# Attention weights times v in blocks of 64 keys on either half of the partitions, each half for its own queries

## The chip, the cores and the metric

The kernel runs on one NeuronCore of a Trainium2 chip. Its engines are TensorE (PE in the profile, with weight loads as PEld), VectorE (DVE), ScalarE (ACT), GpSimd (POOL) and SyncE (SP, which here only issues transfers). The metric is the device time of one execution in microseconds. Three runs of the kernel before took 1031.42, 1033.16 and 1033.86 us, median 1033.16.

## The reference

Attention with a threshold for 8 batches of 8 heads, 576 tokens and 64 values a head: each query keeps only the keys whose score lies within tau of its best. Then a block with an activation on all 4608 tokens. Everything is float32.

```python
scores = scale * np.matmul(q, k.transpose(0, 1, 3, 2))
thresh = np.max(scores, axis=-1, keepdims=True) - tau
scores = np.where(scores >= thresh, scores, -1000000000.0)
attn = np.exp(scores - np.max(scores, axis=-1, keepdims=True))
attn = attn / (np.sum(attn, axis=-1, keepdims=True) + 1e-09)
attn_out = np.matmul(attn, v)
x = attn_out.transpose(0, 2, 1, 3).reshape(4608, 512)
h = x @ w_in                                   # 512 -> 1024
solu = h * softmax(h)
ln = (solu - mean) / np.sqrt(var + 1e-06) * g_ln
out = ln @ w_out                               # 1024 -> 512
```

## The kernel before, in words

**Units and slots.** Two heads that lie next to each other are a pair (hp, four a batch). A unit is one pair with 256 queries (kind 0 or 1), or, as kind 2, the last 64 queries of all four pairs of a batch: nine units a batch, 72 in all. A unit is made in two slots of 128 queries (r = 0, 1), so there are 144 slots, and the main loop (line 764) runs one round a slot and some more at the end. Everything is written out in program order (manual_schedule); each engine takes its instructions in that order.

**A round's scores.** TensorE writes the scores of the slot's two heads into the PSUM tiles s0 and s1 (line 414). VectorE takes each row's maximum (430) and makes the threshold of it (434), ScalarE pushes what is below the threshold far down (443) and takes the exponential with its sum (453), GpSimd divides by the sum in the round after (460 to 463). Before the scores, in the same PSUM tiles, stand items: transposes of q, k or the second block's u by TensorE (282), at most seven of 64 columns.

**Turning the weights.** The product with v needs keys on the partitions. VectorE's transpose turns 32x32 blocks only (475): a row group of 32 queries stays where it is, and T holds, for each of the 18 key blocks, 32 keys by 32 queries. T has two buffers. When both slots of a unit are turned, SP issues 16 transfers (485) that move blocks to other partitions: the 18 key blocks are cut into four runs of 4 or 5 (STARTS, COUNTS), run c goes to partitions 32c to 32c + 31, for each of the four query groups a. In wT, then, four blocks of keys stand on 128 partitions, at five places j, of which the fifth is filled for one half of the partitions only.

**The product with v.** attend (491) multiplies on the four 64x64 quadrants of TensorE: the row half r holds keys, the column half h is the head. For each j there are up to four matmuls of 64 keys by 256 queries (516), 18 a unit; for the fifth place (j = 4, with v's tail in its own tile ve) only the row half z has keys. Each half of the keys collects its sum in a PSUM bank of its own. In the next round attended (522) brings the two together: ScalarE copies the lower half's sum to xh (537), VectorE adds the upper half's (538). Only then do the two banks of this PSUM tile return to the list pairs_free, which holds two tiles, p0 and p1, for all of pv, h_ps and o_ps.

**The second block.** A tile of 128 tokens takes four quarters, one a round: h_ps in two (569), then o_ps of the tile before in two (674). After the second quarter VectorE takes the row maximum hm (582), ScalarE the exponential u (588), VectorE the product (594) and later the statistics (604); TensorE turns u in the rounds after (282). After the last slot both products are made in the plain form (560, 665) with tp_u (645) as the transpose of u. Output goes out by SP (704).

**What sets the order around the change.** A unit whose second slot is s is due for its product in round s + LAG_PV (709); the loop (816) takes it when no tile is in work or the quarter is one of the two with h_ps. In a group of four rounds, then, two units are multiplied in the h_ps rounds, after h_ps. A new tile is taken up in the round after its last unit's product. blocks for slot s stand in round s + 1, at its end. SP's queue holds, in program order, block transfers, outputs and the loads of q, k and v of the next batch (load_at, 731).

Of the kernel before, what the change touches and what calls it, by code (L numbers as in the profile page):

```python
# [8 lines left out]
F32 = mybir.dt.float32  # L9
# [11 lines left out]
def kernel(  # L21
# [63 lines left out]

    STARTS = ((0, 5, 10, 14), (0, 4, 8, 13))
    COUNTS = ((5, 5, 4, 4), (4, 4, 5, 5))

    halves = {}
    ends = {}  # L90
    tails = {}
    pairs = {}
# [47 lines left out]
    def load_v(b, hf):  # L140
        d = halves.setdefault((b, hf), {})
        hs = slice(4 * hf, 4 * hf + 4)
        d["v"] = loads.tile([P, 4, 4, D], F32, tag="v", bufs=3, name="v")
        nc.sync.dma_start(
            out=d["v"].rearrange("p h t d -> p h (t d)"),
            in_=v[b, hs, 0:SM, :].rearrange("h (p t) d -> p h (t d)", t=4),
        )

        if hf == 0:
            tails[b] = loads.tile([P, 4, D], F32, tag="ve", name="ve")  # L150
        nc.sync.dma_start(
            out=tails[b][ROWS[hf]], in_=v[b, hs, SM:S, :].rearrange("h p d -> p h d")
        )

# [47 lines left out]
    def weight_a(x):  # L202
        if not wide:
            return
        d = raws[x]
        hi = d["raw"].bitcast(I32).rearrange("p (n two) -> p n two", two=2)[:, :, 1]
        d["em"] = e, m = [work.tile([P, 512], I32, tag="em", bufs=4, name="em") for _ in range(2)]
# [83 lines left out]
    def source(i):  # L291
        b, hp = divmod(i, NP)
        return halves[b, hp // 2], 2 * (hp % 2)
# [32 lines left out]
    def k_parts(i):  # L326

        kT = pair(i)["kT"]
        z = i % NP // 2
        lo, hi = (kT[:, 0:256], kT[:, 256:S]) if z else (kT[:, 0:320], kT[:, 320:S])  # L330
        lo, hi = (a.rearrange("p (c x) -> p c x", c=2) for a in (lo, hi))
        last = (lo, hi)[z][:, :, P : P + 32]
        return [a[:, :, 0:P].rearrange("p c (j k) -> p j c k", j=4) for a in (lo, hi)], last

    def k_item(i, ts=slice(0, 4)):
        src, h0 = source(i)
        to, _ = k_parts(i)
        n = ts.stop - ts.start
# [5 lines left out]
        def keep(spare, x, r):  # L344
            (nc.vector.tensor_copy if r and not spare.get("eased") else nc.scalar.copy)(
                out=to[r][:, ts],
                in_=seen(spare, r, x, n).rearrange("p t (c k) -> p t c k", c=2),
            )
# [3 lines left out]
    def e_item(i):  # L352
        src, h0 = source(i)
        _, last = k_parts(i)

# [111 lines left out]
    def blocks(s):  # L467
# [8 lines left out]
        if r == 0:  # L476
            return
        u["wT"] = wT = work.tile([P, 4, 5, 2, 2, 32], F32, tag="wT", bufs=3, name="wT")
        for step in range(4):
            for c in range(4):  # L480
                a = (c + step) % 4

                z = hp // 2 if kind < 2 else a // 2
                m, n = STARTS[z][c], COUNTS[z][c]
                nc.sync.dma_start(
                    out=wT[32 * c : 32 * c + 32, a, 0:n].rearrange("p j r h x -> p (j r h x)"),
                    in_=T[32 * a : 32 * a + 32, m : m + n].rearrange("p j r h x -> p (j r h x)"),
                )


    def attend(key):
# [4 lines left out]
        _, y = unit["y"]  # L496
        ve = tails[b]

        for p in range(NP) if kind == 2 else [hp]:
            d, h0 = source(b * NP + p)  # L500
            z, e = divmod(p, 2)
            for j in (0, 4, 1, 2, 3):
                for r in range(2):
                    if j == 4 and r != z:
                        continue
                    for h in range(2):
                        if kind == 2:
                            o = 512 * r + 64 * p
                            to = y[ROWS[h], o : o + 64].rearrange("p (a x) -> p a x", a=2)
                            rhs = wT[ROWS[r], 2 * z : 2 * z + 2, j, e, h]  # L510
                        else:
                            to = y[ROWS[h], 512 * r : 512 * r + 256].rearrange(
                                "p (u a x) -> p a u x", u=2, a=4
                            )
                            rhs = wT[ROWS[r], :, j, :, h]
                        nc.tensor.matmul(  # L516
                            out=to,
                            lhsT=ve[ROWS[r], h0 + h] if j == 4 else d["v"][ROWS[r], h0 + h, j],
                            rhs=rhs, start=j == 0, stop=j == 3,
                        )  # L520

    def attended(key):
        b, kind, hp = key
        tag, y = units.pop(key)["y"]
        lo, hi = y[:, 0:256], y[:, 512:768]
        if kind == 2:
            if b % 2 == 0:
                xe[b // 2] = work.tile([P, NP, P], F32, tag="xe", name="xe")
            to = xe[b // 2][:, :, 64 * (b % 2) : 64 * (b % 2) + 64]
            lo, hi = (a.rearrange("p (h x) -> p h x", h=NP) for a in (lo, hi))  # L530
        else:
            if hp == 0:
                xh[b, kind] = work.tile(
                    [P, NP, 256], F32, tag=f"xh{(2 * b + kind) % 4}", bufs=1, name="xh"
                )
            to = xh[b, kind][:, hp]
        nc.scalar.copy(out=to, in_=lo)  # L537
        nc.vector.tensor_tensor(out=to, in0=to, in1=hi, op=ALU.add)  # L538
        pairs_free.append(tag)
# [168 lines left out]
    PER = NS // B  # L708
    LAG_PV = 4

# [28 lines left out]
    with tc.manual_schedule():  # L739
# [24 lines left out]
        while True:  # L764
# [54 lines left out]
            if quarter == 0 and cur is not None:  # L819
                ff_h(cur, 0, rnd + 1 < NS)  # L820
                quarter = 1
            elif quarter == 1:
                ff_h(cur, 1, None)
# [3 lines left out]
                middle.setdefault(rnd + 3, []).append(lambda t=cur: ff_stats(t))  # L827
            elif quarter == 2 or (quarter == 0 and prev is not None):
                if prev is None or (ffn[prev].get("turned") == 2 and w2_done):
                    if prev is not None:  # L830
                        ff_o(prev, 0, rnd + 1 < NS)
                    quarter = 3
            elif quarter == 3:
                if prev is not None:
# [67 lines left out]
```

## Time and profile before

| | |
|---|---|
| median of 3 runs | 1033.16 us |
| profiled execution | 1034.9 us, span of the instructions 1033.1 us |
| mean granted TensorE clock | 0.964 |
| TensorE busy | 924.1 us, 16251 matmul records |
| VectorE, ScalarE, GpSimd busy | 713.9, 593.0, 470.6 us |
| transfers on SP's and the other queues | 133.63 MB |

A line of the groups gives the source line, engine, operation, names (out <- in), partitions x elements and count, then busy time, mean length of one in ns, and the engine's idle time before them with what ended it. Every float32 matmul is two records. Busy time of TensorE is the time in which at least one record is in flight, so it says nothing of how many of the four quadrants work. A line of the waits has who waited <- for whom, microseconds in total, times, and the longest. A line of the timeline has the start in the span, the length, the engine and the instruction; x8 means eight merged. A line of the stretches gives the stretch, its length, then busy time and instruction count of PE, PEld, DVE, ACT and POOL, the granted clock, the share of the transfer engines and GB/s.

### The profile page before, as it was taken

To read this page: it belongs to the slowest core of one execution; us is meant where nothing else is said; L and a number is where in the kernel's file an instruction comes from. 1 tells how busy PE (TensorE), PEld (TensorE's weight loads), DVE (VectorE), ACT (ScalarE), POOL (GpSimd) and SP (SyncE) were. 2 spreads that over 40 slices of the span, in tenths; PEclk is the share of its full clock that TensorE was granted. 3 is DMA by queue.
4 is the path that set the end of the run, shared out by engine and by line. 5 is a ranking of instruction groups with operands and counts; after the bars stand their busy time and mean duration, and the time that the engine had idled before them with its cause. 6 is when DMAs were issued, how large, how long until landed. Compare 5 with 4: busy or idle time off the path is not lost. (4 is left out here: it accounts for less than half of the span.)

```text
span 1033.1 us, 38699 instructions
## 1 busy us (share of the span) xinstructions
PE 924.1 (89%) x16251; PEld 580.0 (56%) x16251; DVE 713.9 (69%) x1369; ACT 593.0 (57%) x1291; POOL 470.6 (46%) x899
## 2 busy tenths in 40 slices
PE   5566679989989999989999999999989999999997
PEld 3244337657755566556665566556656566555443
DVE  5887977777765776677766776777767777776231
ACT  5776746656655665566655665656656566655111
POOL 3766745445433444434534444444534445545011
PEclk9667799999999999999999999999999999999999
DMA  7766435554545445554645445464545544444200
GB/s 234 180 199 188 103 93 139 157 136 103 147 124 156 112 114 149 148 136 107 153 121 162 117 113 139 122 171 111 138 111 167 129 115 108 127 114 115 76 21 20
DMA packets 101357, 133.63 MB, mean 129 GB/s; under 512 B 33080, under 2 KB 57664, under 8 KB 101184
## 3 DMA queue, kind: packets, MB, share of 16 engines
q1 hardware_dynamic: 99952, 129.19, 48.0%
q8 instruction: 128, 2.10, 0.9%
q10 hardware_dynamic: 1232, 1.97, 0.6%
q14 instruction: 45, 0.37, 0.1%
HBM read 36.70 MB, written 9.44 MB: 45 GB/s over the span
## 5 line engine op out<-in xcount | busy, mean ns | idle before, releaser
L443 ACT ACTIVATE w<-s_ps,nth 128x576 f32<-128x576 f32 x288 | 213.2, 741 | 260.3 <-DVE nth L434 212.4
L475 DVE STREAM_TRANSPOSE T<-w 128x576 f32<-128x576 f32 x288 | 204.9, 750 | 99.5 <-DMA wT<-T 50.4
L674 PE MATMUL o_ps<-w,uT 64*64 64x256 f32 x3968 | 232.4, 381 | 22.0 <-DVE xh L538 17.6
L430 DVE TENSOR_REDUCE nm<-s_ps 128x1 f32<-128x576 f32 x288 | 215.8, 749 | 50.0 <-PE s_ps L414 49.5
L674 PEld LDWEIGHTS o_ps<-w,uT 64*64 64x64 f32 x3968 | 158.9, 134 | 114.7 <-DVE xh L538 39.5
L463 POOL TENSOR_SCALAR w<-w,sm 128x576 f32<-128x576 f32 x288 | 215.3, 760 | 14.4
L453 ACT ACTIVATE w<-w,ntau 128x576 f32<-128x576 f32 x288 | 219.4, 766 | 0.0
L569 PE MATMUL h_ps<-w,xh 64*64 64x512 f32 x1856 | 216.3, 596 | 1.2 <-POOL mark L106 1.0
L414 PE MATMUL s_ps<-kT,qT 64*64 64x64 f32 (+1 forms) x2048 | 175.5, 435 | 25.2 <-ACT w L443 17.0
L516 PE MATMUL pv<-wT,v 64*64 64x256 f32 (+1 forms) x3072 | 183.8, 334 | 15.1 <-DMA wT<-T 12.3
L516 PEld LDWEIGHTS pv<-wT,v 64*64 64x64 f32 x3072 | 131.4, 137 | 75.9 <-issue 47.5
L569 PEld LDWEIGHTS h_ps<-w,xh 64*64 64x64 f32 x1856 | 99.7, 135 | 105.2 <-issue 88.2
L460 POOL TENSOR_SCALAR sm<-sm 128x2 f32<-128x2 f32 x144 | 36.5, 254 | 260.9 <-ACT w L453 257.8
L461 POOL TENSOR_TENSOR sm<-sm,mone 128x2 f32<-128x2 f32 x144 | 104.8, 728 | 12.0
L588 ACT ACTIVATE u<-h_ps,hm 128x1024 f32<-128x1024 f32 x36 | 40.1, 1114 | 82.5 <-DVE hm L582 82.3
L106 POOL MEMSET mark<- 128x1 f32 x63 | 6.3, 99 | 155.5 <-PE o_ps L674 153.6
L414 PEld LDWEIGHTS s_ps<-kT,qT 64*64 64x64 f32 x2048 | 57.4, 142 | 33.4 <-ACT w L443 22.7
L538 DVE TENSOR_TENSOR xh<-xh,pv 128x256 f32<-128x256 f32 x64 | 26.9, 420 | 70.9 <-ACT xh L537 70.8
L434 DVE TENSOR_SCALAR nth<-nm,tau_t 128x1 f32<-128x1 f32 x288 | 61.7, 214 | 10.2
L282 PEld LDWEIGHTS s_ps<-ident,u 64*64 64x64 f32 x1984 | 50.4, 136 | 19.4 <-ACT w L443 6.0
L282 PE MATMUL s_ps<-ident,u 64*64 64x64 f32 x1984 | 53.9, 224 | 8.2 <-ACT w L443 4.6
L453 ACT ACTIVATION_READ_ACCUMULATOR w<-w,ntau 128x1 f32 x288 | 55.3, 192 | 0.0
(95 smaller groups left out, 889.4 us busy)
## 6 DMA issues: line engine op xcount, KB each, us to landing
wT<-T SPq DMA_DIRECT2D x576, 80.0 KB, 2.1
wT<-T SPq DMA_DIRECT2D x576, 64.0 KB, 2.0
v<-in_v_dram SPq DMA_DIRECT2D x16, 512.0 KB, 4.6
out_dram<-ob SPq DMA_DIRECT2D x32, 256.0 KB, 3.4
q<-in_q_dram SPq DMA_DIRECT2D x15, 512.0 KB, 4.7
k<-in_k_dram SPq DMA_DIRECT2D x15, 512.0 KB, 7.2
raw<-in_moe_w_out_dram SPq DMA_DIRECT2D x8, 512.0 KB, 4.6
raw<-in_moe_w_in_dram SPq DMA_DIRECT2D x5, 512.0 KB, 4.3
```

The source lines that it names most:

```text
L282: nc.tensor.matmul(out=spare[r][ROWS[y], to], lhsT=lhsT_of(r, y), rhs=ident[ROWS[r], ROWS[r]], start=True, stop=True,)
L414: nc.tensor.matmul(out=ps[h][ROWS[y], ks], lhsT=lhsT, rhs=d["kT"][ROWS[h], ks], start=True, stop=True,)
L430: nc.vector.tensor_reduce(out=nm, in_=ps[:, 0:S], axis=AX.X, op=ALU.max, negate=True)
L434: nc.vector.tensor_scalar(out=nth, in0=nm, scalar1=tau_t, scalar2=None, op0=ALU.add)
L443: nc.scalar.activation(out=w, in_=ps[:, 0:S], func=AF.Prelu, bias=d["nth"][x], scale=1.0, alpha=1.0e30,)
L453: nc.scalar.activation(out=w, in_=w, func=AF.Exp, bias=ntau, scale=1.0, accum_out=sm[:, x : x + 1])
L461: nc.gpsimd.tensor_tensor(out=sm, in0=sm, in1=mone, op=ALU.pow)
L463: nc.gpsimd.tensor_scalar(out=w, in0=w, scalar1=sm[:, x : x + 1], scalar2=1.0, op0=ALU.mult, op1=ALU.mult)
L475: nc.vector.transpose(out=T[:, :, r, h, :], in_=w)
L516: nc.tensor.matmul(out=to, lhsT=ve[ROWS[r], h0 + h] if j == 4 else d["v"][ROWS[r], h0 + h, j], rhs=rhs, start=j == 0, stop=j == 3,)
L569: mm = nc.tensor.matmul(out=h[ROWS[y], f], lhsT=x[ROWS[r], c, ROWS[y]], rhs=w1[ROWS[r], c, f], start=part == 0 and c == 0, stop=part == 1 ...
L674: mm = nc.tensor.matmul(out=o[ROWS[y], 512 * z : 512 * z + 256], lhsT=d["uT"][ROWS[r], c, ROWS[y]], rhs=w2[ROWS[r], c, 256 * z : 256 * z + ...
```

## The change

The nine blocks of 64 keys (NK) now lie one after the other: wT holds, on the lower 64 partitions, all 576 keys for the queries of row groups 0 and 1, and on the upper 64 all keys for the queries of row groups 2 and 3. Two of the transposes' key blocks, m and m + 9, stand on the 64 partitions of a half. kT's columns are laid out so that they come out in this order. That needs 8 transfers a unit instead of 16, each of 32 partitions with 9 blocks. v is loaded twice, once for each half of the partitions, in three transfers a half (six for two before). A unit is 9 x 4 matmuls of 64 keys by 128 queries; the sums of the two halves are of different queries, so ScalarE's copy is all that remains of attended. The units of kind 2 have two pairs on each half and keep 72 matmuls of 64 columns.

LAG_PV is 3 for 4, and the loop decides on the step of the second block first: a product that is due may now stand in any round without an o_ps step.

```diff
@@ load_v
-        d["v"] = loads.tile([P, 4, 4, D], F32, tag="v", bufs=3, name="v")
-        nc.sync.dma_start(
-            out=d["v"].rearrange("p h t d -> p h (t d)"),
-            in_=v[b, hs, 0:SM, :].rearrange("h (p t) d -> p h (t d)", t=4),
-        )
...
+        d["v"] = loads.tile([P, 4, NK, D], F32, tag="v", bufs=3, name="v")
+        for rows in ROWS:
+            for r in range(2):
+                nc.sync.dma_start(
+                    out=d["v"][rows, :, 4 * r : 4 * r + 4].rearrange("p h t d -> p h (t d)"),
+                    in_=v[b, hs, 256 * r : 256 * r + 256, :].rearrange("h (p t) d -> p h (t d)", t=4),
+                )
+            nc.sync.dma_start(
+                out=d["v"][rows, :, NK - 1], in_=v[b, hs, SM:S, :].rearrange("h p d -> p h d")
+            )
@@ k_parts
...
+        return pair(i)["kT"].rearrange("p (c m k) -> p m c k", c=2, m=NK)
@@ blocks
-        u["wT"] = wT = work.tile([P, 4, 5, 2, 2, 32], F32, tag="wT", bufs=3, name="wT")
-        for step in range(4):
-            for c in range(4):
-                a = (c + step) % 4
-                z = hp // 2 if kind < 2 else a // 2
-                m, n = STARTS[z][c], COUNTS[z][c]
+        T = T.rearrange("p (c m) r h x -> p c (m r h x)", c=2)
+        u["wT"] = wT = work.tile([P, 2, NK, 2, 2, 32], F32, tag="wT", bufs=3, name="wT")
+        to = wT.rearrange("p g m r h x -> p g (m r h x)")
+        for a in range(4):
+            for g in range(2):
+                c, first = a % 2, a - a % 2
                 nc.sync.dma_start(
-                    out=wT[32 * c : 32 * c + 32, a, 0:n].rearrange("p j r h x -> p (j r h x)"),
-                    in_=T[32 * a : 32 * a + 32, m : m + n].rearrange("p j r h x -> p (j r h x)"),
+                    out=to[32 * a : 32 * a + 32, g],
+                    in_=T[32 * (first + g) : 32 * (first + g) + 32, c],
                 )
@@ attend
-            for j in (0, 4, 1, 2, 3):
-                for r in range(2):
-                    if j == 4 and r != z:
-                        continue
+        for e in range(2) if kind == 2 else [None]:
+            for m in range(NK):
+                for u in range(2):
                     for h in range(2):
...
+                            to = y[ROWS[h], u, 0:P].rearrange("p (r g x) -> p g r x", r=2, g=2)
+                            rhs = wT[ROWS[u], :, m, :, h]
...
@@ attended
-        nc.scalar.copy(out=to, in_=lo)
-        nc.vector.tensor_tensor(out=to, in0=to, in1=hi, op=ALU.add)
+        nc.scalar.copy(out=to, in_=y)
         pairs_free.append(tag)
@@ main loop
-    LAG_PV = 4
+    LAG_PV = 3
...
+            due = bool(pv_due) and pv_due[0][0] <= rnd
+            step = None
+            if quarter < 2 and cur is not None:
+                step = ("h", quarter)
+            elif quarter == 3:
+                step = ("o", 1)
+            elif quarter == 2 or (prev is not None and not due):
+                if prev is None or (ffn[prev].get("turned") == 2 and w2_done):
+                    step = ("o", 0)
-            if pv_due and pv_due[0][0] <= rnd and (not busy or quarter < 2):
-                if len(pairs_free) > (busy and quarter == 0):
-                    attending = pv_due.pop(0)[1]
+            if due and (step is None or step[0] == "h") and len(pairs_free) > (step == ("h", 0)):
+                attending = pv_due.pop(0)[1]
```

What moves in the order is shown at three places. First SP's queue, in the middle of the program, from a load of v through one unit's block transfers (wT<-T; the sizes are partitions x elements). Before:

```order
L144 DMA v<-in_v_dram 128x4x256
L151 DMA ve<-in_v_dram 64x4x64
L704 DMA out_dram<-ob 128x512
L485 DMA wT<-T 32x640 x2
L485 DMA wT<-T 32x512 x2
L485 DMA wT<-T 32x640 x2
L485 DMA wT<-T 32x512 x2
L485 DMA wT<-T 32x640 x2
L485 DMA wT<-T 32x512 x2
L485 DMA wT<-T 32x640 x2
L485 DMA wT<-T 32x512 x2
```

The same part of SP's queue in the changed kernel, with two units behind the output:

```order
L482 DMA wT<-T 32x1152 x8
L146 DMA v<-in_v_dram 64x4x256 x2
L150 DMA v<-in_v_dram 64x4x64
L146 DMA v<-in_v_dram 64x4x256 x2
L150 DMA v<-in_v_dram 64x4x64
L482 DMA wT<-T 32x1152 x8
L697 DMA out_dram<-ob 128x512
L482 DMA wT<-T 32x1152 x16
```

Sixteen instructions a unit have become eight, and two instructions for a half of v six.

Second, TensorE in the two h_ps rounds of a tile (h_ps is the second block's first product, pv the product with v, s_ps<-ident the items, s_ps<-kT,qT the scores). Before:

```order
L569 MATMUL h_ps<-w_74,xh 64x512 x16
L516 MATMUL pv<-wT,v 64x4x2x32 x4
L516 MATMUL pv<-wT,ve 64x4x2x32 x2
L516 MATMUL pv<-wT,v 64x4x2x32 x12
L282 MATMUL s_ps<-ident,u 64x64 x16
L414 MATMUL s_ps<-kT,qT 64x64 x4
L414 MATMUL s_ps<-kT,qT 64x512 x4
L569 MATMUL h_ps<-w_74,xh 64x512 x16
L516 MATMUL pv<-wT,v 64x4x2x32 x4
L516 MATMUL pv<-wT,ve 64x4x2x32 x2
L516 MATMUL pv<-wT,v 64x4x2x32 x12
```

The same two rounds on TensorE in the changed kernel:

```order
L562 MATMUL h_ps<-w_74,xh 64x512 x16
L510 MATMUL pv<-wT,v 64x2x2x32 x36
L283 MATMUL s_ps<-ident,u 64x64 x16
L410 MATMUL s_ps<-kT,qT 64x64 x4
L410 MATMUL s_ps<-kT,qT 64x512 x4
L562 MATMUL h_ps<-w_74,xh 64x512 x16
L510 MATMUL pv<-wT,v 64x2x2x32 x36
```

The place of the product is the same, after h_ps; its units are those of one round earlier.

Third, TensorE at the end of the slots (s_ps<-kT,qe are the last two slots' scores, o_ps the second product of a tile, tp_u the plain transposes of u). Before:

```order
L414 MATMUL s_ps<-kT,qe 64x64 x4
L414 MATMUL s_ps<-kT,qe 64x512 x4
L674 MATMUL o_ps<-w_75,uT 64x256 x32
L414 MATMUL s_ps<-kT,qe 64x64 x4
L414 MATMUL s_ps<-kT,qe 64x512 x4
L674 MATMUL o_ps<-w_75,uT 64x256 x32
L645 MATMUL tp_u<-ident,u 128x128 x8
L560 MATMUL h_ps<-w_74,xh 128x512 x4
L516 MATMUL pv<-wT,v 64x4x2x32 x4
```

And in the changed kernel:

```order
L410 MATMUL s_ps<-kT,qe 64x64 x4
L410 MATMUL s_ps<-kT,qe 64x512 x4
L667 MATMUL o_ps<-w_75,uT 64x256 x32
L283 MATMUL s_ps<-ident,u 64x64 x16
L410 MATMUL s_ps<-kT,qe 64x64 x4
L410 MATMUL s_ps<-kT,qe 64x512 x4
L553 MATMUL h_ps<-w_74,xh 128x512 x4
L510 MATMUL pv<-wT,v 64x2x2x32 x36
L638 MATMUL tp_u<-ident,u 128x128 x4
```

One half of an o_ps and half of its tile's transposes of u now stand ahead of the last scores.

More of the change, by code (lines that the diff above doesn't have):

```diff
@@ L206, in weight_a @@
         hi = d["raw"].bitcast(I32).rearrange("p (n two) -> p n two", two=2)[:, :, 1]
-        d["em"] = e, m = [work.tile([P, 512], I32, tag="em", bufs=4, name="em") for _ in range(2)]
+        d["em"] = e, m = [
+            work.tile([P, 512], I32, tag=t, bufs=n, name="em") for t, n in (("em", 2), ("m", 1))
+        ]
         nc.vector.tensor_scalar(
@@ L353, in e_item @@
         src, h0 = source(i)
[L354 removed]
+        last = k_parts(i)[:, NK - 1]
         def make(spare, x):
@@ L827 @@
                 middle.setdefault(rnd + 3, []).append(lambda t=cur: ff_stats(t))
[L828 to L833, printed above, removed]
+            elif step == ("o", 0):
+                if prev is not None:
+                    ff_o(prev, 0, rnd + 1 < NS)
+                quarter = 3
+            elif step == ("o", 1):
                 if prev is not None:
```

54 lines of the change are left out of this document (18 added, 36 removed).

## The prediction, made before the run

> **What bounds the kernel now.** I read the page's busy rows first, then the busy time by stage, the waits, and the timeline of single rounds. A round is the work for one slot; four rounds carry one token tile of the second block (two with h_ps, then two with o_ps), and two units are multiplied in the h_ps rounds.
>
> ```profile
> PE 924.1 (89%) x16251; PEld 580.0 (56%) x16251; DVE 713.9 (69%) x1369; ACT 593.0 (57%) x1291; POOL 470.6 (46%) x899
> PE   5566679989989999989999999999989999999997
> DVE  5887977777765776677766776777767777776231
> ```
>
> TensorE is the fullest engine and nearly all its slices are full from the seventh on, while VectorE is at 7 or 8 there. By stage (start to round 28, rounds 28 to 143, tail after the last scores):
>
> ```profile
> 0.00:202.14 202.14, 146.71 (x2378) 93.52 (x2382) 154.76 (x293) 128.98 (x281) 114.90 (x179) 0.84 0.59 160
> 202.14:943.75 741.61, 697.76 (x13406) 447.49 (x13401) 532.39 (x1038) 448.10 (x981) 340.29 (x682) 0.99 0.51 131
> 943.75:1033.00 89.25, 79.69 (x484) 38.96 (x476) 26.75 (x40) 15.86 (x30) 15.45 (x39) 1.00 0.18 48
> ```
>
> The middle holds 741.61 us for 115 rounds, 25.8 us for a group of four. How short can a group be? The score matmuls (L414) start every round, so their starts give the rounds:
>
> ```profile
> 357.16 1.18 PE L414 MATMUL s_ps<-kT,qe 64*64 64x64 f32 x16
> 358.14 3.63 PE L569 MATMUL h_ps<-w,xh 64*64 64x512 f32 x32
> 361.57 0.63 PE L516 MATMUL pv<-wT,v 64*64 64x256 f32 x8
> ...
> 364.15 1.19 PE L414 MATMUL s_ps<-kT,qe 64*64 64x64 f32 x15
> ```
>
> ```profile
> 529.11 1.17 PE L414 MATMUL s_ps<-kT,qT 64*64 64x64 f32 x16
> 534.09 0.23 PE L414 MATMUL s_ps<-kT,qT 64*64 64x64 f32 x2
> 538.99 0.23 PE L414 MATMUL s_ps<-kT,qT 64*64 64x64 f32 x2
> ```
>
> An undisturbed h_ps round took 6.99 us (scores 0.98, h_ps 3.43, then a unit and what prepares the next scores), two undisturbed o_ps rounds 4.98 and 4.90. A group of these is 23.9. So 1.9 us a group, about 55 us in 28.75 groups, are stops of a TensorE that is otherwise full. Who stops it:
>
> ```profile
> PEld o_ps L674 <- DVE xh L538: 39.5, 26, 2.3
> PE o_ps L674 <- DVE xh L538: 17.6, 22, 1.4
> PE s_ps L414 <- ACT w L443: 17.0, 13, 4.1
> PE pv L516 <- DMA wT<-T: 12.3, 14, 2.8
> PE pv L516 <- issue: 2.8, 7, 0.6
> DVE T L475 <- DMA wT<-T: 50.4, 40, 5.3
> ```
>
> Two stops stand out: o_ps waits until the add of the halves gives its banks free, and pv waits for the block transfers. The change touches both.
>
> **The change part by part.**
>
> *Block transfers, 16 to 8 a unit, used one round earlier.* This is how pv came to wait at 524 us, with SP's rows beside it (start, length) and the sizes:
>
> ```profile
> 504.49 1.43 DVE L475 STREAM_TRANSPOSE T<-w 128x576 f32<-128x576 f32 x2
> 508.47 0.58 SPq L131 DMA_DIRECT2D q<-in_q_dram  x1
> 510.48 0.64 SPq L136 DMA_DIRECT2D ends<-in_k_dram  x1
> 511.24 12.43 SPq L485 DMA_DIRECT2D wT<-T  x16
> 524.06 0.65 PE L516 MATMUL pv<-wT,v 64*64 64x256 f32 x4 [1.69 <-DMA wT<-T]
> 957.31 10.00 SPq L485 DMA_DIRECT2D wT<-T  x16
> wT<-T SPq DMA_DIRECT2D x576, 80.0 KB, 2.1
> wT<-T SPq DMA_DIRECT2D x576, 64.0 KB, 2.0
> v<-in_v_dram SPq DMA_DIRECT2D x16, 512.0 KB, 4.6
> L516 PE MATMUL pv<-wT,v 64*64 64x256 f32 x2048 | 164.2, 392 | 15.1 <-DMA wT<-T 12.3 <-issue 2.8
> ```
>
> The blocks were ready at 505.92, but SP issued earlier work until 511.24, and then these until 523.67: 12.43 us for 16, 10.00 where little else runs (0.625 each). Two rounds are 12.9 us, so SP is nearly full and its backlog is the wait. With 8 issues a unit takes SP 5.0 us; 147 KB lands, by the 2.1 us for 80 KB and the 4.6 for 512 (0.006 us per KB), in about 2.5: 7.5 us from transposed to usable. The room shrinks too. For the unit used soonest, three rounds after its slot, the transposes end about where the first h_ps round starts, and pv comes in the second, 6.99 + 0.98 + 3.43 = 11.4 us later. 3.9 us are spare, so I let this wait vanish. Its price now: 12.3 + 2.8 us idle, and in each of the 21 stops the last record's pipe must drain besides (0.39 us long, 3.43 / 64 = 0.05 apart, so 0.34), 22 us. I take **-20**, between 0 and -22. v's loads cost SP 64 issues more, at 0.625 some 40 us over the whole run against 360 taken off, and 9.4 MB more move where the transfers' engines are 0.51 busy. I put that at nothing: spare SP time covers it. If that cover is gone, the last rival prices it.
>
> [...]
>
> *No sum of halves.* The wait of o_ps, in one round:
>
> ```profile
> 656.11 1.44 DVE L475 STREAM_TRANSPOSE T<-w 128x576 f32<-128x576 f32 x2 [1.57 <-DMA wT<-T]
> 657.47 1.19 DVE L582 TENSOR_REDUCE hm<-h_ps 128x1 f32<-128x1024 f32 x1
> 658.26 1.19 PE L414 MATMUL s_ps<-kT,qT 64*64 64x64 f32 x16
> 658.69 1.11 ACT L588 ACTIVATE u<-h_ps,hm 128x1024 f32<-128x1024 f32 x1 [1.78 <-DVE hm L582]
> 659.79 0.36 ACT L537 COPY xh<-pv 128x256 f32<-128x256 f32 x1
> 660.19 0.42 DVE L538 TENSOR_TENSOR xh<-xh,pv 128x256 f32<-128x256 f32 x1 [1.54 <-ACT xh L537]
> 660.67 1.53 PE L674 MATMUL o_ps<-w,uT 64*64 64x256 f32 x24 [1.23 <-DVE xh L538]
> ```
>
> Read from the bottom: o_ps waits for the add, that for ScalarE's copy, that for the exponential, that for VectorE's maximum, and that for a transpose which waited 1.57 us for a transfer to leave its T buffer. The add alone is worth 660.61 - 660.15 = 0.46 us a time. The rest needs the T wait gone. With the transfers done 7.5 us after the transposes, not some 18 (505.92 to 523.67), a T buffer is free when its turn comes. Then the maximum follows h_ps at once, and from its start to the copy's end these rows show 2.7 us (657.47 to 660.15). With the last record's 0.6 that is 3.3 to 3.4, while TensorE has the unit, the items and the scores for about 3.5. So nothing is late in its place by more than a few tenths. Price now: 17.6 us idle and 22 drains of 0.34, 25 us; the weight loads' 39.5 bounds it from above. Sure are 26 x 0.46 = 12. I take **-20**, between -12 and -28. Elsewhere the 72 adds (30 us of VectorE) are off the path.
>
> *36 matmuls of 128 columns for 18 of 256.* Now the fifth key block of a half fills two of four quadrants. What records cost beside the rows above:
>
> ```profile
> 510.18 0.64 PE L282 MATMUL s_ps<-ident,u 64*64 64x64 f32 x32
> ```
>
> Each matmul is two records. From 361.57 to 364.15 lie one unit and 32 records of 64 columns; those are (0.64 - 0.23) / 31 = 13.2 ns apart (0.23 us is two records, above), 0.42 us, so the unit takes 2.16. h_ps shows 3.43 / 32 = 107 ns for 512 columns, thus 53.6 for 256 and 26.8 for 128, if records stay in proportion, as 13.2 for 64 says they do. 72 x 26.8 = 1.93 us, 0.23 less; over 64 units 15 us. I take **-10**, as some stops now hide part of it; bounds 0 to -15, with the loss side in a rival. The units of end queries keep 72 matmuls of 64 columns.
>
> [...]
>
> *Order of the rounds.* One round less of lag starts the second block one round earlier, and one quarter leaves the tail:
>
> ```profile
> 944.73 3.63 PE L674 MATMUL o_ps<-w,uT 64*64 64x256 f32 x64
> 948.29 0.65 PE L645 MATMUL tp_u<-ident,u 128*128 128x128 f32 x4
> ```
>
> 3.56 + 0.65 us leave a stage that is a chain; they come back in the start, where TensorE is busy 146.71 of 202.14 us. **-4.** In the start, SP's relief brings raw weights sooner, and v's doubled load competes: **-2**, from -8 to +6.
>
> *What comes late next.* VectorE has 532.39 / 28.75 = 18.5 us of work in a group, 0.84 less without two adds: 17.7 of about 23.5, so it is no bound on the whole. But the o_ps rounds have under 5 us, and in the first of them VectorE also holds the key copies and u's product. I give back **+5** (29 groups at 0.2), up to +15.
>
> Sum: -20 - 20 - 10 - 4 - 2 + 5 = -51. The profiled execution took 1034.9 us (span 1033.1), 1.7 above the median of the runs; 1034.9 - 51 = 983.9, and by that 1.7 less, **982 us**.
>
> **The rivals.**
>
> *Half of it.* The maximum stays late for another reason, so o_ps gains only the 12 us of the add, and the uneven VectorE takes back 15: 8 + 10 worse, 1000 us. For it: behind T's wait for a transfer may stand one for POOL, hidden now; against: 40 of T's waits end with the transfers.
>
> *More.* The stops of scores on ACT (17.0) go as well and nothing is given back: 982 - 17 - 5 = 960. For it: VectorE loses 30 us of work; against: 4.1 of these 17.0 are one wait, so they are not a steady part of the rounds.
>
> *Slower: a record's cost doesn't follow its columns.* If a 128-column record takes the 53.6 ns of a 256-column one, because its weight load sets the pace, a unit takes 3.86 us, 1.7 more; 64 of these are 109, and 982 + 10 + 109 = 1101. It decides above 26.8 + 41 / (64 x 72) us, that is 36 ns a record. Against it stand the 13.2 ns of records with loads of the same 64x64 size.
>
> *Slower: the blocks land too late for one round less.* If eight bigger transfers take as long as sixteen now (12.4 + 2.1 us), they exceed the room of 11.4 by 3.1 in each group; 29 of these are 90, 1072 us. It turns into a loss from 1.8 us of waiting, a chain of 13.2. [...] Against: SP's issue took 0.58 and 0.64 us for loads of several times the size.
>
> That the change doesn't do what it says I leave out: the order of instructions shows eight transfers and no add.
>
> **How the numbers follow.** The forecast has 0.56, half of it 0.20, more 0.12, each slower rival 0.05, no change 0.02. A measurement of this kernel can tell about 0.2% from no change. Faster is 0.56 + 0.20 + 0.12 = 0.88, slower 0.10, same 0.02. The forecast's own range, with pv's, the start's and the give-back's bounds partly together, is 966 to 997; with "half" and "more" it reaches 957 to 1008, which leaves out the slower rivals and the far ends.
>
> **What would show it.** Right: pv no longer waits for wT, and T hardly for wT; 8 issues a unit in about 5 us on SP; o_ps behind ACT's copy with a few us in total; pv records of 128 columns some 27 ns apart and 2 us a unit; groups of four rounds near 24 us; a tail near 85. Wrong: pv waiting for wT in every second h_ps round, records over 36 ns, or groups still above 25 us with VectorE or ScalarE at the end of the scores' wait.

## The result and the profile after

| | before | after |
|---|---|---|
| median (lowest to highest of 4 runs) | 1033.51 us (1031.42 to 1034.97) | 964.51 us (962.67 to 966.33) |
| profiled execution, its span | 1034.9 us, 1033.1 | 966.33 us, 964.4 |
| start / middle / tail of that span | 202.14 / 741.61 / 89.25 us | 203.16 / 677.90 / 83.34 us |

The ratio is 0.9334, with a 95% interval of 0.9307 to 0.9361: faster by 69 us, where 51 were forecast. Two of e4_rec64's ten executions below (1044.36 and 1047.86 us) and one of e_best2's four (3234.21 us) were slower than the rest of their kernel and are left out of its median.

The busy rows of the changed kernel's page:

```profile
PE 892.6 (93%) x18583; PEld 647.8 (67%) x18583; DVE 692.1 (72%) x1298; ACT 593.0 (61%) x1291; POOL 473.2 (49%) x899
PE   4467678999999999999999999999999999999997
```

TensorE is now at 9 in every slice from the eighth to the one before the last. Where before it had slices of 8 all over the middle, none is left. The three stages (first column of numbers the length, then busy time and instructions of TensorE, its weight loads, VectorE, ScalarE, GpSimd, then the granted clock, the transfers' share and GB/s):

```profile
0.00:203.16 203.16, 144.07 (x2873) 94.74 (x2877) 154.85 (x284) 130.01 (x284) 117.55 (x177) 0.83 0.74 180
203.16:881.06 677.90, 673.53 (x15240) 515.98 (x15236) 511.90 (x978) 447.38 (x980) 340.31 (x684) 1.00 0.64 151
881.06:964.40 83.34, 75.03 (x498) 37.03 (x488) 25.38 (x37) 15.59 (x30) 15.30 (x38) 0.99 0.18 48
```

The middle gave 63.7 us, the tail 5.9, and the start took 1.0. In the middle TensorE is busy 673.53 of 677.90 us. The waits that answer to those of before (in all, times, longest):

```profile
DVE nm L426 <- PE s_ps L410: 164.1, 109, 3.5
PE pv L510 <- DMA wT<-T: 13.5, 6, 4.9
PEld o_ps L667 <- ACT xh L531: 10.7, 25, 1.0
DVE T L471 <- DMA wT<-T: 8.4, 41, 0.6
```

T waited 50.4 us for the transfers and now 8.4; o_ps waited 39.5 for VectorE and now 10.7 for ScalarE's copy. VectorE in turn waits 164.1 us for TensorE's scores: the order of who is late has turned round. The 13.5 us of pv all lie in the start. A group of four rounds in TensorE's timeline (start, length), with SP's two rows:

```profile
453.83 1.19 PE L410 MATMUL s_ps<-kT,qe 64*64 64x64 f32 x14
454.75 3.70 PE L562 MATMUL h_ps<-w,xh 64*64 64x512 f32 x32
458.18 2.23 PE L510 MATMUL pv<-wT,v 64*64 64x128 f32 x72
460.15 0.68 PE L283 MATMUL s_ps<-ident,u 64*64 64x64 f32 x30
...
477.63 0.76 PE L410 MATMUL s_ps<-kT,qT 64*64 64x64 f32 x10
```

```profile
453.94 5.68 SPq L482 DMA_DIRECT2D wT<-T  x8
465.63 6.05 SPq L482 DMA_DIRECT2D wT<-T  x8
```

From 453.83 to 477.63 the group takes 23.8 us, against 25.8 on average before. A unit lasts 460.15 - 458.18 = 1.97 us, 27.4 ns for each of its 72 records. SP needs about 6 us for a unit's transfers and has most of the next 6 free.

One view that the prediction did not show says the same more plainly: the waits of SP's own queue, of before and then of after.

```profile
SPq L485 <- DVE T L475: 14.9, 6, 3.5
```

```profile
SPq L482 <- DVE T L471: 311.1, 70, 10.0
```

Before, SP waited for a unit's transposes only six times, 14.9 us in the whole run; it always had older work. Now it waits for 70 of 72 units, 311.1 us. In the middle alone the lengths of its issues add up, in the traces, to 673 of 741.61 us before and to 395 of 677.90 after.

### The profile page after: what moved, and what is told of

Same layout as the page of the kernel before. It is cut to its first block, busy times and chain, and to the rows that moved or that the text cites. A ratio compares the mean times of both kernels' runs of the same rounds, so it can differ in the third digit from the quotient of the medians.

```text
span 964.4 us, 42893 instructions
## 1 busy us (share of the span) xinstructions
PE 892.6 (93%) x18583; PEld 647.8 (67%) x18583; DVE 692.1 (72%) x1298; ACT 593.0 (61%) x1291; POOL 473.2 (49%) x899
## 3 DMA queue, kind: packets, MB, share of 16 engines
q10 hardware_dynamic: 1232, 1.97, 0.7%
## 5 line engine op out<-in xcount | busy, mean ns | idle before, releaser
L426 DVE TENSOR_REDUCE nm<-s_ps 128x1 f32<-128x576 f32 x288 | 216.4, 751 | 164.9 <-PE s_ps L410 164.1
L667 PEld LDWEIGHTS o_ps<-w,uT 64*64 64x64 f32 x3968 | 195.0, 134 | 50.7 <-issue 15.7
L510 PEld LDWEIGHTS pv<-wT,v 64*64 64x64 f32 x5760 | 166.4, 137 | 49.9 <-issue 41.9
L510 PE MATMUL pv<-wT,v 64*64 64x128 f32 (+1 forms) x5760 | 169.4, 265 | 15.0 <-DMA wT<-T 13.5
L410 PE MATMUL s_ps<-kT,qT 64*64 64x64 f32 (+1 forms) x2048 | 170.4, 425 | 8.8 <-ACT w L439 7.2
L562 PEld LDWEIGHTS h_ps<-w,xh 64*64 64x64 f32 x1856 | 110.1, 134 | 91.1 <-issue 82.7
L456 POOL TENSOR_SCALAR sm<-sm 128x2 f32<-128x2 f32 x144 | 39.4, 274 | 264.1 <-ACT w L449 261.1
L575 DVE TENSOR_REDUCE hm<-h_ps 128x1 f32<-128x1024 f32 x36 | 43.0, 1193 | 17.6 <-PE h_ps L553 17.5
L283 PEld LDWEIGHTS s_ps<-ident,u 64*64 64x64 f32 x2016 | 46.8, 136 | 10.3 <-ACT qT L316 4.1
L283 PE MATMUL s_ps<-ident,u 64*64 64x64 f32 x2016 | 48.8, 221 | 4.8 <-ACT qT L316 2.4
```

The lines of the kernel that those rows point to most:

```text
L283: nc.tensor.matmul(out=spare[r][ROWS[y], to], lhsT=lhsT_of(r, y), rhs=ident[ROWS[r], ROWS[r]], start=True, stop=True,)
L410: nc.tensor.matmul(out=ps[h][ROWS[y], ks], lhsT=lhsT, rhs=d["kT"][ROWS[h], ks], start=True, stop=True,)
L426: nc.vector.tensor_reduce(out=nm, in_=ps[:, 0:S], axis=AX.X, op=ALU.max, negate=True)
L510: nc.tensor.matmul(out=to, lhsT=d["v"][ROWS[u], h0 + h, m], rhs=rhs, start=m == 0, stop=m == NK - 1,)
L562: mm = nc.tensor.matmul(out=h[ROWS[y], f], lhsT=x[ROWS[r], c, ROWS[y]], rhs=w1[ROWS[r], c, f], start=part == 0 and c == 0, stop=part == 1 ...
L667: mm = nc.tensor.matmul(out=o[ROWS[y], 512 * z : 512 * z + 256], lhsT=d["uT"][ROWS[r], c, ROWS[y]], rhs=w2[ROWS[r], c, 256 * z : 256 * z + ...
```

## The experiments

My theory after the result: SP's issuing alone held up the middle, so that every wait there (pv's, T's, and through T and the maximum that of o_ps) was SP's time in another place. The rivals: the absent add, the cheaper matmuls, or the new order of the rounds carried the gain, or the bytes did. Four kernels change before in one respect, the others the changed kernel.

**Eight of sixteen transfers alone (b_eight).** Before, with eight of a unit's sixteen transfers left out, so that half of the weights' places, now in three fixed buffers zeroed at the start, keep zeros and old numbers:

```
-        for step in range(4):
+        for step in range(2):
```

> The kernel before with eight of the sixteen transfers of each unit left out (half of the weights' places keep zeros, and what they held); matmuls, add and lag as before. Theory A (SP's backlog is the cause of the pv waits, of T's lateness and through it of the late add): the pv waits and T's wait go, and most of the 39.5 us ahead of o_ps: 975 to 990 us, so nearly the whole gain with the add still in. Theory B (the add has its own part of 12 to 30 us): 995 to 1010 us.

Measured: 964.0 us, ratio 0.9306 (0.9275 to 0.9337). That is the changed kernel's time, with the add, the wide matmuls, the lag of four and the old loop all still in. It went past the range given for theory A, and B's is far off. That the two medians lie within 1 us is partly chance: in the sum further down the other parts give 6.2 us and take 9.6. Its middle and its waits:

```profile
191.58:871.66 680.08, 677.36 (x13406) 491.48 (x13402) 533.65 (x1037) 447.21 (x981) 339.37 (x683) 1.00 0.35 91
```

```profile
PEld o_ps L677 <- DVE xh L541: 16.1, 26, 1.1
DVE T L478 <- DMA wT<-T: 1.8, 10, 0.2
PEld pv L519 <- DMA wT<-T: 0.5, 2, 0.2
```

The middle lost 61.5 of the 63.7 us. The wait of o_ps for the add fell from 39.5 to 16.1 without the add being touched.

**The add alone (b_copyonly).** Before, without the VectorE add; only the first half's sums reach the output:

```
-        nc.vector.tensor_tensor(out=to, in0=to, in1=hi, op=ALU.add)
```

> The kernel before with the VectorE add of a unit's two halves left out (only the first half's sums reach the output); all else, sixteen transfers among it, as before. Theory A (the add stands late because VectorE is held by its wait for T's transfers; the backlog on SP is the cause): the wait ahead of o_ps goes, 15 to 30 us of 39.5, but it comes back in part as a wait of pv for wT, since the rounds are now shorter and SP is still behind: 1010 to 1030 us. Theory B, the prediction's (12 us of the add's own time, sure in themselves): 1015 to 1021 us. Theory C (the add alone carried the gain): below 1000 us.

Measured: 1032.1 us, ratio 0.9968 (0.9941 to 0.9996), 3 us. B and C fall; A's size was also too large. The wait was not taken away, it moved:

```profile
DVE T L475 <- DMA wT<-T: 88.0, 50, 6.0
PEld o_ps L673 <- ACT xh L537: 29.8, 23, 1.8
```

T's wait grew from 50.4 to 88.0 us, and o_ps waits 29.8 us for ScalarE's copy, which is late behind VectorE's maximum and so, by the chain that the prediction read, behind T. The middle took 741.73 us, as before.

**Sixteen issues, fewer bytes (b_half16).** Taking eight transfers away takes bytes away too. Here all sixteen stay, each of two blocks, and the other places keep zeros:

```
-                m, n = STARTS[z][c], COUNTS[z][c]
+                m, n = STARTS[z][c], COUNTS[z][c] // 2
```

> The kernel before with its sixteen transfers a unit, each of only two blocks for its four or five (the weights' other places keep zeros), so the same number of issues and 44% of the bytes; all else as before. Theory (SP's issues, some 0.63 us each whatever their size, are the bound of the whole middle): 1025 to 1036 us. Rival (bytes, or the time that packets take to land): near the 964 us of the kernel with eight of the sixteen left out.

Measured: 1021.59 us, ratio 0.9899 (0.9873 to 0.9925). So about 12 us come with the bytes (8 of them in the middle), 3 more than I allowed, and the other 57 with the number of issues; the changed kernel, which has all the bytes and eight issues, has b_eight's middle within 2.2 us. SP's wait for T stays small:

```profile
SPq L488 <- DVE T L478: 17.9, 8, 3.5
```

**A third T buffer (b_T3).** To make room, the start's em gives up one of its four buffers, as it does in the change:

```
-            units[key] = dict(T=work.tile([P, NB, 2, 2, 32], F32, tag="T", name="T"))
+            units[key] = dict(T=work.tile([P, NB, 2, 2, 32], F32, tag="T", bufs=3, name="T"))
```

> The kernel before with three buffers for T in place of two (the start's em in a smaller place to make room, as the change has it). Theory (SP has no time left, so every wait only moves to another place): VectorE's wait for T goes and pv's wait for wT grows, 1026 to 1036 us. Rival (a chain of waits through T, the late add and o_ps, with time left on SP): 1000 to 1015 us.

Measured: 1030.79 us, ratio 0.9976 (0.9944 to 1.0008), no difference. Yet the chain that the prediction read is gone from its waits:

```profile
PE pv L518 <- DMA wT<-T: 22.6, 16, 4.4
PEld o_ps L676 <- DVE xh L540: 10.2, 19, 1.1
DVE T L477 <- DMA wT<-T: 1.7, 9, 0.2
```

T's wait fell from 50.4 to 1.7 and that of o_ps from 39.5 to 10.2, and pv's grew from 12.3 to 22.6. The chain was read rightly and had no price of its own.

**Sixteen issues in the changed kernel (e3_sixteen, e3_lag4).** Each transfer is cut in two, the second kernel with LAG_PV = 4 besides:

```
-                nc.sync.dma_start(
-                    out=to[32 * a : 32 * a + 32, g],
-                    in_=T[32 * (first + g) : 32 * (first + g) + 32, c],
-                )
+                for js in (slice(0, 640), slice(640, 1152)):
+                    nc.sync.dma_start(
+                        out=to[32 * a : 32 * a + 32, g, js],
+                        in_=T[32 * (first + g) : 32 * (first + g) + 32, c, js],
+                    )
```

> The changed kernel with each of a unit's eight block transfers cut in two (blocks 0 to 4 and 5 to 8): sixteen issues on SP again, the same bytes, smaller packets. Theory (SP's issue time is the chain): sixteen issues at 0.6 us take 10 us, the last lands 12.5 us after the transposes where the earlier pv has 11.4, and a backlog grows: pv waits 1 to 4 us in half of the units, T is late again, the time is 980 to 1000 us. Rival (bytes and partition lines in flight make the chain, not issues): 8 or 16 are alike, 962 to 968 us.

> The changed kernel with sixteen half transfers a unit (1106 us with a lag of three rounds), and a lag of four. Theory (SP has no time left in the middle): a later start of pv buys little, 1080 to 1106 us. Rival (the time from the transposes to usable weights is the limit, 12 to 17 us against 11.4 of room, and a round more covers it): 1000 to 1045 us.

Measured: 1105.96 us, ratio 1.0724 (1.0662 to 1.0786), and 1087.34 us, ratio 1.0546 (1.0492 to 1.0601). The first is 106 us worse than my upper end: I had added waits to rounds, and a queue without spare time does not work like that. The second fell inside the theory's range and far from the rival's. Their middles:

```profile
225.29:1021.14 795.85, 711.29 (x15235) 549.05 (x15231) 512.21 (x978) 449.86 (x979) 340.34 (x684) 0.95 0.54 130
```

```profile
213.30:996.08 782.78, 710.01 (x15243) 494.67 (x15237) 511.42 (x980) 447.54 (x982) 339.26 (x681) 0.97 0.55 134
```

Counting SP's transfers in the middle of each trace gives one number for all slow kernels:

| kernel | issues by SP in the middle | middle, us | us per issue |
|---|---|---|---|
| before | 1005 | 741.61 | 0.74 |
| b_T3 | 1004 | 737.01 | 0.73 |
| b_half16 | 1008 | 733.66 | 0.73 |
| b_copyonly | 1005 | 741.73 | 0.74 |
| e3_lag4 | 1055 | 782.78 | 0.74 |
| e3_sixteen | 1049 | 795.85 | 0.76 |
| after | 586 | 677.90 | 1.16 |
| b_eight | 540 | 680.08 | 1.26 |

With over 1000 issues the middle is the count times 0.73 to 0.76 us; from one issue's start to the next SP most often took 0.63 us (the median), and the rest are longer ones. That is also, for the most part, why these two are slower than before: v twice adds 48 issues to the middle, which at 0.74 are 36 us, of the 41 between before and e3_lag4 there and of the 54 between before and e3_sixteen. The rest of the 54 stays open; in the middle of e3_sixteen SP waited 17 us for transposes.

**Two queues (e_twoq).** The same sixteen halves, the second ones issued by GpSimd:

```
-                for js in (slice(0, 640), slice(640, 1152)):
-                    nc.sync.dma_start(
+                for queue, js in ((nc.sync, slice(0, 640)), (nc.gpsimd, slice(640, 1152))):
+                    queue.dma_start(
```

> The kernel with sixteen half transfers a unit, but eight of them issued by POOL's queue and eight by SP's. Same packets and bytes as with all sixteen on SP (1106 us). Theory (the issue time of one queue is the chain): back to 962 to 985 us, the upper part if POOL's issues hold its own work up. Rival (smaller packets and more of them make the transfers late): 1080 us and above.

Measured: 1055.31 us, ratio 1.0185 (1.0153 to 1.0217): neither range. Its waits tell why (mark is the memset on GpSimd that orders TensorE's two halves of h_ps):

```profile
PE pv L511 <- DMA wT<-T: 3.0, 3, 1.7
POOL wT L483 <- DVE T L471: 99.6, 60, 3.7
PEld h_ps L563 <- POOL mark L104: 71.8, 29, 4.9
PE h_ps L563 <- POOL mark L104: 46.8, 26, 4.0
DVE T L471 <- POOL w L459: 68.6, 47, 5.8
```

In e3_sixteen the same packets, all issued by SP, made pv wait much longer:

```profile
PE pv L511 <- DMA wT<-T: 89.0, 33, 4.6
PEld pv L511 <- DMA wT<-T: 32.3, 15, 4.9
```

And SP's own wait for the transposes in e_twoq:

```profile
SPq L483 <- DVE T L471: 356.6, 70, 10.4
```

A weight load and its matmul wait partly at the same time (the 89.0 and 32.3 us of e3_sixteen are 93.5 when counted once); so counted, pv's wait fell with half of the issues elsewhere from 93.5 to 3.6 us, and SP waited 356.6 us for transposes where it had waited 34.1 in e3_sixteen: the issues were the cause, not the packets' size. But GpSimd now stands in its queue until VectorE has transposed (99.6 us in 60 waits), issues for 4 us (8 at 0.51), and its fence and its scaling of the weights come behind that. The price was 71.8 us in which h_ps's weight loads, and for 46.8 of them its matmuls too, waited for the fence.

**The add put back (e2_add).** In the changed kernel:

```
         nc.scalar.copy(out=to, in_=y)
+        nc.vector.tensor_tensor(out=to, in0=to, in1=y, op=ALU.max)
```

> The changed kernel with the VectorE step put back: after ScalarE's copy of a unit's result, VectorE takes the maximum of that copy and the same numbers in PSUM (as wide as the old add; the result stays the same), and frees the buffer. Theory: the o_ps groups behind it wait again for VectorE, 26 to 30 of them by the add's own 0.46 us, 12 to 14 us: 974 to 982 us, and pv does not wait. Rival (the add alone made the whole wait of 39.5 us ahead of o_ps): 25 to 35 us, 990 to 1000 us. Second rival (the add lay beside other work): within 2 us of 964.5.

Measured: 965.94 us, ratio 0.9356 (0.9317 to 0.9395), 1.4 us more than without it, which the intervals do not tell apart: the second rival. The middle took 681.62 us, 3.7 more, and the start 2.3 less. VectorE, with 164 us of waiting for scores, had room for it.

**Matmuls of 64 columns (e4_rec64).** A unit in 144 matmuls in place of 72 (the two slots of a unit one after the other):

```
-        for e in range(2) if kind == 2 else [None]:
+        for e in range(2):
```

> The changed kernel with weights times v in 144 matmuls of 64 columns a unit for 72 of 128, the same products. Theory (a record costs its columns): records 13.5 to 14 ns apart, 1.95 to 2.05 us a unit, 962 to 970 us. [...]

Measured: 1034.12 us, ratio 1.0006 (0.9979 to 1.0032), 70 us more than after and above the theory's 962 to 970, for a reason that it did not have. Its middle, and two of its rounds on TensorE:

```profile
204.37:944.07 739.70, 693.44 (x18912) 523.70 (x18908) 512.14 (x978) 447.89 (x980) 340.31 (x684) 1.00 0.59 139
```

```profile
534.18 2.31 PE L506 MATMUL pv<-wT,v 64*64 64x64 f32 x142
536.27 0.23 PE L283 MATMUL s_ps<-ident,u 64*64 64x64 f32 x2
...
541.15 1.90 PE L506 MATMUL pv<-wT,v 64*64 64x64 f32 x113
545.15 0.63 PE L506 MATMUL pv<-wT,v 64*64 64x64 f32 x28 [2.10 <-issue]
```

The first unit runs nearly as the theory had it: 536.27 - 534.18 = 2.09 us for 142 records, 14.7 ns each. In the second TensorE stops for 2.1 us, and nothing that the profile knows released it. Such stops are all over, not at pv alone; in the middle, 61.8 us longer than after, they are 45.2 us of the trace, and TensorE's busy time is 19.9 more:

```profile
PE s_ps L283 <- issue: 25.2, 19, 2.1
PE pv L506 <- issue: 15.9, 14, 3.0
PE s_ps L410 <- issue: 7.1, 5, 2.5
```

The page's list of DMA queues has one that brings instructions (packets, MB, share):

```profile
q8 instruction: 183, 3.00, 1.2%
```

That is 183 pieces of 16 KB here; the changed kernel's page has 147, that of before 128, for 18583 and 16251 records of TensorE. By 147 pieces for 2 x 18583 matmuls and weight loads a piece holds some 250 of these, by estimate. All 24 stops of over 0.8 us with no releaser, after the start, end 1.2 to 1.7 us after such a piece has landed. So I take it that TensorE was waiting for its program; no run changed that supply alone.

**A lag of four (e1_lag4), and two attempts on top of it (e_best, e_best2).**

```
-    LAG_PV = 3
+    LAG_PV = 4
```

e_best has four rounds for all but the last two units, e_best2 four for the first batch's units and three for all later ones; both load g_rows ahead of v (e_best's line first, then e_best2's, then the load):

```
-            pv_due.append((s + LAG_PV, (b, kind, hp)))
+            pv_due.append((s + (4 if s + 4 < NS else 3), (b, kind, hp)))
...
-            pv_due.append((s + LAG_PV, (b, kind, hp)))
+            pv_due.append((s + (4 if b == 0 else 3), (b, kind, hp)))
...
+        nc.sync.dma_start(out=g_rows, in_=g_ln.rearrange("(c p) -> c p", p=P))
         load_v(0, 0)
         load_v(0, 1)
-        nc.sync.dma_start(out=g_rows, in_=g_ln.rearrange("(c p) -> c p", p=P))
```

> The changed kernel with one edit: weights times v may start four rounds after its unit's second scores, as before the change, and no longer three. Theory (eight issues on SP in place of sixteen, no VectorE add, T free sooner carry the gain): the middle stays within 3 us of its 677.9, since the weights are in place in time at either lag; the tail grows by 4 to 6 us, because the last unit is one round later; the start may win back up to 8 of the 13.5 us that PE waits there for wT. Sum 957 to 969 us. Rival (the new order of the rounds carries it): 10 us or more come back, 975 us and above.

> The changed kernel with a lag of four rounds for all but the last two units, three for these, and g_rows loaded ahead of v. Expected: the middle as with a lag of four (675 us), the tail as with three (83.3 us), and the start shorter by the 4.8 us that PE waits for g_rows: 946 to 952 us. Rival (the start is bound by ScalarE's work on the first scores, and the wait for g_rows only stands in its place): 951 to 957 us.

> The changed kernel with a lag of four rounds for the first batch's nine units and three for all later ones, and g_rows loaded ahead of v. Expected: start 188 to 191 us up to the 29th round (203.2 in the changed kernel), middle 676 to 679, tail 83 to 84, so 949 to 954 us. Rival (the lag of three costs in the middle what it saves in the tail): 957 us and above.

Measured: 956.86 us, ratio 0.9265 (0.9217 to 0.9314); 958.5 us, ratio 0.9254 (0.9212 to 0.9295); 960.34 us, ratio 0.9316 (0.9247 to 0.9386). The first has its middle and tail as expected and ends 0.1 us below its range, by a start that won 12.5 us where up to 8 were expected; with the second it is the fastest of all. The second missed its range and its rival's, the third fell into its rival's. The three stages of e1_lag4, then the middle of e_best2:

```profile
0.00:190.71 190.71, 138.85 (x2778) 94.02 (x2782) 152.77 (x282) 129.60 (x282) 116.59 (x178) 0.87 0.78 192
190.71:866.05 675.34, 671.39 (x15240) 519.55 (x15236) 508.40 (x979) 447.26 (x980) 339.48 (x683) 1.00 0.64 152
866.05:954.80 88.75, 79.14 (x556) 39.93 (x548) 25.82 (x37) 16.10 (x32) 15.38 (x39) 1.00 0.17 45
```

```profile
190.62:874.40 683.78, 676.99 (x15336) 513.42 (x15332) 512.58 (x979) 447.88 (x981) 340.77 (x684) 1.00 0.63 150
```

The lag of four shortens the start by 12.5 us and the middle by 2.6, and lengthens the tail by 5.4. With three, the first units' pv stands in TensorE's queue ahead of the next scores while their blocks are on the way; so in the changed kernel's timeline:

```profile
41.22 0.69 PE L510 MATMUL pv<-wT,v 64*64 64x128 f32 x4 [4.91 <-DMA wT<-T]
43.79 3.48 PE L510 MATMUL pv<-wT,v 64*64 64x128 f32 x60 [1.88 <-DMA wT<-T]
```

In e1_lag4, in place of the 13.5 us of pv in six waits:

```profile
PE pv L510 <- DMA wT<-T: 0.9, 1, 0.9
```

In e_best2 the middle grew by 8.4 us against e1_lag4, which is more than the 5.4 that its tail saved (83.30 us): the quarter of a tile that leaves the tail is done in the middle, with 96 records more. e_best kept the long tail, 88.78 us, so the last two units alone do not set it; e_best2's tail says that the place of the whole run of tiles does. Its earlier g_rows shortened the start by 2.4 us, less than the medians can tell.

## Why the prediction was right or wrong, point by point

**The sum.** By spans: before to b_eight -72.1 us; from there to e1_lag4, which adds the new matmuls, v twice, the new loop and no add, -6.2; from there to after, the lag of three, +9.6. Together -68.7. The prediction split its -51 otherwise. These are spans of one execution each; by the ratios (0.9306, 0.9265, 0.9334) the last two steps are 4 and 7 us, and the intervals overlap, so their sizes are rough, and -6.2 also holds the cost of the bytes that b_eight leaves out. That the total missed by only 18 us is partly luck: fewer issues gave 30 us more than the terms that stood for them (-20, -20 and -2), and the lag, at +9.6 for -4, took 14 of these back.

**Block transfers, -20, and o_ps, -20.** The signs were right, and so was SP's backlog as the cause: pv no longer waits in the middle, T hardly, o_ps 10.7 us in all, and SP needs 6 us a unit where 5 were said. The sizes were wrong together: 40 against 61.5 us in the middle and 10.6 in the start, both from b_eight. The step that failed is "The add alone is worth 660.61 - 660.15 = 0.46 us a time" and, from it, "Sure are 26 x 0.46 = 12". The add was the last in a chain whose first member was SP, and a step that stands last in a chain is worth only what its removal does not hand on: b_copyonly gave 3 us, e2_add took 1.4. In the same way the bounds of -22 and -28 were taken from the idle time ahead of two operations. Here the row that decides was SP's own: 14.9 us of waiting for T in 1033. The text did say that SP "is nearly full and its backlog is the wait", but then priced the waits one by one and not the queue. Had it priced the queue, the middle would have been TensorE's own time without stops: 28.75 groups of the 23.9 it had worked out are 687 us, 55 below 741.61, where 61.5 came. That v's added issues cost nothing was right with eight transfers a unit, since SP has the time; with sixteen they were 36 us of the middle.

**36 matmuls of 128 columns, -10.** The length was right (27 ns a record and 2 us a unit forecast; 27.4 and 1.97 measured), the worth was smaller, though inside its bounds of 0 to -15: the matmuls, the absent add and all else but the lag gave 4.7 us of middle together, 680.08 to 675.34. The slower rival had asked whether a weight load sets the pace; 14.7 ns for a record of 64 columns in e4_rec64, where 128 took 27.4, answers no. But a loss exists one doubling further, by what I take for the supply of instructions, which the prediction did not have in view: 144 matmuls a unit cost 70 us, with 45 us of such stops in the middle, and 72 left one stop of 1.5 us.

**Order of the rounds, -4, and the start, -2.** The tail went as said (85 forecast, 83.34 measured). The start came out 1.0 us longer, inside the -8 to +6 given for it, but by chance: b_eight's halved issues took 10.6 us off it, and the lag of three put 12.5 on, which the prediction did not have. With +2.6 in the middle and -5.4 in the tail the lag alone is +9.6, where -4 was said: this step failed. The prediction took the start's idle TensorE for a place where the moved quarter is free, and did not ask whether the transfers of the first units, with v's twelve loads and the weights' on the same queue, would land within one round less. The room of 11.4 us was worked out for the middle alone. (The start's em, with three buffers for four, is no large part: b_T3, which has the same, started in 203.56 us against 202.14.)

**What comes late next, +5.** Nothing did: groups take 23.8 us, and VectorE, with two adds less a group, waits 164.1 us for scores. The second slower rival, a chain over 13.2 us, did not come about with eight transfers: 6 us of issue and the 3.2 to land that the page gives are 9. With sixteen it did, and there it cost more than the rival said.

**The rivals.** "More" at 960 was nearest, though the scores' wait for ScalarE that it names fell only from 17.0 to 7.2 us: the number came near for another reason. "Half of it" had a maximum that stays late; b_T3 shows that it was late through T's transfers.

What stays open: why e2_add's start is 2.3 us shorter than that of after, how much of the last 4.7 us of middle is matmuls and how much the add, and what the 19.9 us more of busy time in e4_rec64 are (busy time runs to the end that the profile models for a record, for those of pv in after 213 to 472 ns past the start).

## What to carry to other kernels

When several waits lead back to one queue, look at that queue's own waits first: if it hardly ever waits for its producer, its count of issues times the time of one comes near the length of the stage (in before 1005 at a median of 0.63 us, so 633 of 742), and what stands behind it is worth little until the count falls (here 3 us for the add, nothing that can be told from noise for a buffer, 13 us of a 796 us middle for a round more of lag). Price such a change as the stage without stops, not as the sum of idle times. And a lag that fits the steady state is to be tried apart in the start, where the same queue still carries the first loads (here three rounds in place of four cost 12.5 us).

## What the runs showed of the hardware that was not expected

- An issue on SP takes 0.63 us (median, from start to start) for 32 KB (b_half16) as for 144 KB (after); over 1000 of them in the middle came to 0.73 to 0.76 us each in six kernels.
- A transfer issued by GpSimd held that engine for 0.51 us (291.4 us for 576):

```profile
L483 POOL DMA_DIRECT2D wT<-T x576 | 291.4, 513 | 115.6 <-DVE T L471 99.6 <-issue 11.4 <-DVE nm L426 3.6
```

- Instructions come in 16 KB pieces, more of them with more records of TensorE (128 for 16251 in before, 147 for 18583 after), never less than 3.3 us apart in e4_rec64 or after. By the estimate of 250 instructions a piece that is 27 ns for a matmul and its weight load, and so just the pace of 128-column records in 64x64 tiles (27.4). The records of 64 columns in e4_rec64 ran faster for a while (14.7 ns) and then the engine stopped, for up to 3.0 us.
- The granted clock was lower in the two kernels whose TensorE stood idle longest in the middle (0.95 with 84.6 us in e3_sixteen, 0.97 with 72.8 in e3_lag4); in e4_rec64, idle for 46.3 us, it was 1.00. What decides it no run shows. Nearly the same records (15240 and 15235) kept TensorE busy 673.53 us after and 711.29 us in e3_sixteen. Busy time holds the modelled ends of records before each stop, so this need not all be the clock.
